# Tiles 2 and 3 of the attention's result turned by DMA instead of TensorE, and a new order of the casts at the head of a transformer block's last MLP passage

## Chip, cores and metric

One core of a Trainium2 chip. The time is that of one execution on the device in microseconds (us), the median of several runs. Five engines work side by side, each through its own queue in program order: PE (TensorE, matmuls and PE transposes), DVE (VectorE), ACT (ScalarE), POOL (GpSimd) and SP (SyncE, which issues nearly all DMAs). Semaphores tie the queues together. PEld is PE's loading of weights, which overlaps its matmuls.

## The reference

```python
x = A_x                                   # 1 x 2048 x 512, fp32
n = layernorm(x)
q, k, v = split(n @ wqkv)                 # 32 heads of 16
# each row looks at 8 rows: itself and those 2, 4, ... 14 before it
w = softmax(q . k[s - 2*i] / 4)           # i = 0..7, rows before 0 masked
h = x + (sum_i w_i * v[s - 2*i]) @ wo
r = relu(layernorm(h) @ w1 + b1)          # 512 -> 1792
out = h + (r * r) @ w2 + b2               # 1792 -> 512
```

## The kernel before

The 2048 rows are 16 tiles of 128. Every fp32 matrix product is made of three products of rounded halves (`mm3`): a value is cast to `hi` (L152, mostly on ACT), the rest `lo = value - hi` is made by L155 on DVE or POOL, and PE adds hi x hi, hi x lo and lo x hi. A product of 128 x 512 over 512 is thus 12 matmuls of 512 columns.

**First phase** (L231 `mm<-big,xh`: q, k and v, tiles 4 to 15 in calls of two). Each call is cut into 12 slots; `k` counts them over the last calls, and in the slots of the two last calls stand the other chores: `OT` the slots in which a tile's attention result is turned, `WO` those of its product with wo, `HK` and `HT` those of the normalised rows `hn`. `at(n, f)` puts f on the list that runs at the start of the slot's end, n slots on, and `after(n, f)` on the one that runs behind that.

**Attention** is a generator in steps of two tiles, run by DVE (L344 q x k, L380 sum, L357 weight x v), ACT (exp L403, the copy `qp` L271) and POOL (the add-up tree L414, three instructions a time, the last writes `o`). `pump()` emits its next piece when a modelled time of DVE has fallen behind a modelled time of PE; so less modelled work on PE moves attention's pieces in the order of every engine.

**Turning.** wo's product and the MLP want tiles with rows on the free axis. Tiles 0 to 3 of `o` are turned by PE: `o_T` makes four PE transposes with `ident` into a PSUM tile `tr` (L204), and hi and lo are cast out of it. Tiles 4 to 15 go by DMA: `o_split` copies `o` on ACT into two planes of 16-bit halves (`pl<-o`, L627), `turn_dma` issues a transposing DMA on SP (`o<-pl`, L631), `o_join` copies the halves back on ACT (again `pl<-o` in the trace, L636), and then come the hi cast (L152, ACT) and lo (L155, DVE). The normalised rows `hn` of most tiles go the same way.

**MLP.** Passages u = 0, 1, 2 of four tiles each (512 columns): for 14 blocks of the hidden layer, `mlp1` (L231 `mm<-big_l,w_h`), relu and square on ACT (`r`, L885 and L886), `rh` (ACT), `rl` (POOL), and `mlp2` (L915 `acc`) three slots later. Between them stand the wo products and norms of the next passage's tiles (L672 `h`, L163/L164 statistics on DVE; L169 to L172 `rs` on POOL). The last passage (tiles 12 to 15) takes its hidden blocks in pairs, seven products instead of eight (`products_a`, `products_b`, L832, 256 columns). For it `t_sums` and `t_split` make sums of w1's blocks (`traw`, `th`, `tl`), and `split_last` makes sums of the turned tiles: `s` (L767, L768, L776, L777 on DVE), cast into `a_h` and `a_l`, which lie in `big_l` and in wo's old place (`wo_h`, `wo_l` in the rows). The part products go through ACT copies `p` (L845, L847) and DVE sums `u` (L846).

Of the kernel before, what the change touches and what calls it, by code (L numbers as in the profile page):

```python
# [20 lines left out]
RI = 2  # L21
# [19 lines left out]
WO = 7, 9, 13, 15  # L41
HT = 20, 20, 21, 23
HK = (12, 18), (14, 19)
W2 = (18,)
LH = 3, 4, 10, 11
OP = 6, 7, 12, 13
# [12 lines left out]
def block_kernel(ctx, tc, x, wqkv, wo, w1, b1, w2, b2, out):  # L59
    nc = tc.nc  # L60
# [55 lines left out]
    def after(delta, fn, *a):  # L116
        late.setdefault(now["slot"] + delta, []).append((fn, a))
# [18 lines left out]
    def dve(t):  # L136
        now["dve"] += t
# [13 lines left out]
    def hi(dst, src):  # L151
        nc.scalar.copy(dst, src)  # L152

    def lo(eng, dst, src, h):
        eng.tensor_tensor(out=dst, in0=src, in1=h, op=ALU.subtract)  # L155
# [447 lines left out]
    def o_T(t):  # L603
        s, j = divmod(t, RI)
        pump(until=s)
        tr = transposes(o_t[s][:, j, :])
        if t % R == RI:

            ohl = att.tile([P, 2, KB, P], F32R, name="ohl", tag="o", bufs=3)
            oT[t] = ohl[:, 0], ohl[:, 1]  # L610
        else:
            oT[t] = row("oh", (P, KB, P), F32R), row("ol", (P, KB, P), F32R)
        at(0, hi_T, tr, [oT[t][0]])
        at(0, lo_T, tr, [oT[t][0]], [oT[t][1]])
# [116 lines left out]
    a_h, a_l = {}, {}  # L731
    s32 = {}
# [14 lines left out]
    def split_last(i, tr):  # L747
        hs_, ls_ = [a[:, :, i] for a in hh], [a[:, :, i] for a in hl]
        if i < RI:
            hi_T(tr, hs_)  # L750
            lo_T(tr, hs_, ls_)
            return
        j = i - RI
        tr0 = last_tr[j]
        if not j:
            a_h.update({2: hh[0][:, :, RI:], **{m: wo_h[:, m % 4].rearrange(
                "p (k i c) -> p k i c", k=2, i=RI) for m in (1, 3, 4)}})
            a_l.update({2: hl[0][:, :, RI:], **{m: wo_l[:, m % 4].rearrange(
                "p (k i c) -> p k i c", k=2, i=RI) for m in (1, 3, 4)}})
            for m in range(1, 5):  # L760
                s32[m] = row("s").rearrange("p (k i c) -> p k i c", k=2, i=RI)
        sm = {m: s32[m][:, :, j] for m in (1, 2)}
        sub, add = ALU.subtract, ALU.add
        tt = nc.vector.tensor_tensor
        a21 = tr[:, :2]
        hi(hs_[1], tr[:, 2:])
        tt(out=sm[1], in0=tr[:, 2:], in1=a21, op=add)  # L767
        tt(out=sm[2], in0=sm[1], in1=tr0[:, :2], op=sub)  # L768
        lo(nc.vector, ls_[1], tr[:, 2:], hs_[1])
        hi(a_h[2][:, :, j], sm[2])  # L770
        lo(nc.vector, a_l[2][:, :, j], sm[2], a_h[2][:, :, j])
        if not j:
            return
        hi(a_h[1], s32[1])
        for j in range(RI):
            tt(out=s32[3][:, :, j], in0=last_tr[j][:, :2], in1=last_tr[RI + j][:, :2], op=sub)  # L776
            tt(out=s32[4][:, :, j], in0=last_tr[j][:, 2:], in1=s32[2][:, :, j], op=sub)  # L777
        for m in (3, 4):
            hi(a_h[m], s32[m])
        for m in (1, 3):  # L780
            lo(nc.vector, a_l[m], s32[m], a_h[m])


    tw = {}
# [20 lines left out]
    def t_split(n):  # L805
        h, l = t_tile(n, "th", F32R), t_tile(n, "tl", F32R)
        hi(h, tw[n])
        for k, eng in ((2, nc.gpsimd), (0, nc.vector if n in (1, 2) else nc.gpsimd)):
            lo(eng, l[:, k:k + 2], tw[n][:, k:k + 2], h[:, k:k + 2])
        tw[n] = h, l  # L810

# [26 lines left out]
    def products_a(n):  # L838
        b = {m: psum.tile([P, D], F32, name="mm", tag=tag)[:, :HD]
             for m, tag in zip((1, 4, 2, 3), XB)}  # L840
        pu = row("p"), row("u")
        pairs[n] = b, pu
        for m, bank in ((1, 1), (4, 4), (6, 2), (5, 3)) if not n else ((1, 1), (6, 2), (5, 3), (4, 4)):
            product(n, m, b[bank], True, m == 4)
        nc.scalar.copy(pu[0][:, :HD], b[1])  # L845
        nc.vector.tensor_tensor(out=pu[1][:, :HD], in0=b[2], in1=pu[0][:, :HD], op=ALU.add)  # L846
        nc.scalar.copy(pu[0][:, HD:], b[3])  # L847

# [153 lines left out]
    for n in range(16):  # L1002
        gp, t = divmod(n, 4)
# [28 lines left out]
    def first_phase(t0):  # L1032
        def chores(m):
            if t0 + 3 < 16:
                if m in (0, 2):
                    at(0, x_stats, t0 + 2 + m // 2)

                early = t0 == 12
                if m + early in ((4, 6) if t0 == R else (6, 7)):
                    at(0, x_norm, t0 + 2 + (m + early) // 7 if t0 > R else t0 + m // 2)  # L1040
                if m in XT[early]:
                    x_T(t0 + 2 + XT[early].index(m))
            if t0 + 5 < 16 and m in (6, 9):
                at(0, load_x, t0 + 2 + m // 3)
            if jobs and m % 3 == 0:
                at(0, weight_job)
            k = t0 // 2 * 12 - 72 + m
            if k == 19:
                dve(HOLD)
            for t in range(R):  # L1050
                if k == OT[t]:
                    at(0, load_h, t)
                    o_T(t)
                if t in HV and k == HK[t][0]:
                    at(0, h_split, t)
                    after(0, turn_dma, ("h", t))
                if t in HV and k == HK[t][1]:
                    at(0, turn_join, ("h", t))
                if k == WO[t]:
                    wo_product(t, (1, 3, 4, 6))  # L1060
                    now["pe"] += 2.73
                if k == HT[t]:
                    (at(0, h_parts, t) if t in HV else h_T(t))
            if k in W2:
                at(0, load_w2, W2.index(k))

        def half(m):
            end_slot(1.37)
            chores(m)

        for n in range(6):
            chores(2 * n)
            qkv_of(t0 + n % 2, n // 2, lambda: half(2 * n + 1))
            end_slot(1.37)
# [40 lines left out]
    for u in range(R - 1):  # L1115
# [10 lines left out]
        todo, halves = {}, {}  # L1126
        for i in js:
            t = R * (u + 1) + i
            if not end:
# [22 lines left out]
                    todo.setdefault(p, []).append(what)  # L1152
                p, h = (HP[i], i % 2) if u < 2 else HL[i]
                if t in HV:
                    todo.setdefault(p - (i == RI and t < 14), []).append(
                        (after if t in (6, 10, 12, 13) else at, 0, h_parts, t))
                else:
                    (todo, halves)[h].setdefault(p, []).append((h_T, t))
            todo.setdefault(UP[i], []).append((at, 0, unspill, R * u + i))
        if u == 2:  # L1160
            for p, *what in ((12, at, 0, t_load, 0), (12, at, 0, t_load, 1), (13, at, 0, t_sums, 0),
                             (13, at, 0, t_sums, 1), (13, at, 1, t_split, 0),
                             (13, at, 1, turn_join, ("h", 15))):
                todo.setdefault(p, []).append(what)

        def half(p):
# [85 lines left out]
    h = hs[S // P - 1]  # L1252
# [34 lines left out]
```

## Time and profile before

| | |
|---|---|
| median of 3 runs | 501.96 us (501.43 to 502.64) |
| the profiled run's own time | 502.12 us |
| its span in the profile | 500.3 us (1.82 us lie outside) |
| PE busy | 495.5 us, 99% |
| DVE / POOL / ACT busy | 383.9 / 356.1 / 306.0 us |
| granted TensorE clock | 1.0 over the span |

The span is the time from the first to the last instruction in the trace. A share of busy time is a mean over the span; what an engine costs is seen at the places where another waits for it.

### The profile page before, as it was taken

What the parts mean: (1) busy time and instruction counts of PE and PEld (TensorE: products, weight loads), DVE (VectorE), ACT (ScalarE), POOL (GpSimd) and SP (SyncE); (2) the same over time, 40 slices, a digit from 0 to 9 for tenths busy, and PEclk for the clock granted to TensorE, in tenths of its full rate; (3) what the DMA queues carried; (4) which work ended last, traced back from release to release, by engine and by line L of the source; (5) the groups of instructions that cost most, each with busy time, mean ns of one, the idle gap of its engine ahead of it and who ended that gap; (6) DMA issues with size and microseconds to landing.
All of it is one profiled execution on the core that took longest, in us unless ns stands there. A gap on an engine that the chain in (4) does not pass through costs nothing.

```text
span 500.3 us, 7521 instructions
## 1 busy us (share of the span) xinstructions
PE 495.5 (99%) x2411; PEld 420.9 (84%) x2411; DVE 383.9 (77%) x524; ACT 306.0 (61%) x544; POOL 356.1 (71%) x430
## 2 busy tenths in 40 slices
PE   8999999999999999999999999999999999999997
PEld 7999888888888888888888888788888888998986
DVE  6479899999989899798989989897984156733233
ACT  5634767668346758387664546766464967766541
POOL 5714798996775999978778777787889353886610
PEclk9999999999999999999999999999999999999999
DMA  9778979989798899679577955977670574355112
GB/s 273 206 207 235 302 239 303 262 275 300 210 229 252 294 284 255 207 209 276 183 254 219 216 144 170 253 238 254 212 201 8 130 198 152 115 159 168 64 43 86
DMA packets 113584, 103.67 MB, mean 207 GB/s; under 512 B 33672, under 2 KB 82056, under 8 KB 113544
## 3 DMA queue, kind: packets, MB, share of 16 engines
q1 hardware_dynamic: 112600, 102.66, 69.9%
q10 hardware_dynamic: 944, 0.52, 0.3%
q8 instruction: 19, 0.31, 0.3%
q14 instruction: 21, 0.17, 0.1%
HBM read 72.65 MB, written 24.25 MB: 194 GB/s over the span
## 4 chain that ended last, share of the span: by engine, by line
PE 94%; ACT 2%; DMA 2%; POOL 1%; DVE 0%; issue 0%; SPq 0%; POOLq 0%
PE mm L231 47%; PE acc L915 28%; PE wo L231 8%; PE mm L832 7%; PE tr L204 2%; DMA o<-pl 2%; PE tr L969 1%; POOL pr L414 1%; ACT pl L627 1%; ACT pl L636 0%; PE half L938 0%; POOL o L414 0%; DVE st L163 0%; DVE h L672 0%; ACT oh L152 0%
## 5 line engine op out<-in xcount | busy, mean ns | idle before, releaser
L414 POOL TENSOR_TENSOR pr<-pr 128x512 f32<-128x512 f32 (+1 forms) x128 | 134.0, 1047 | 34.4 <-DVE pr L357 29.0
L231 PE MATMUL mm<-big_l,w_h 128*128 128x512 f32 x336 | 88.5, 390 | 0.0
L357 DVE TENSOR_TENSOR pr<-ex,v 128x1024 f32<-128x1024 f32 x62 | 75.6, 1221 | 10.3 <-POOL o L414 7.3
L344 DVE TENSOR_TENSOR pr<-qp,k 128x1024 f32<-128x1024 f32 x64 | 76.8, 1200 | 6.1 <-ACT qp L271 3.5
L380 DVE TENSOR_REDUCE ex<-pr 128x64 f32<-128x1024 f32 x64 | 78.4, 1225 | 1.8
L231 PEld LDWEIGHTS mm<-big_l,w_h 128*128 128x128 f32 x336 | 63.0, 188 | 13.4 <-ACT r L885 0.3
L155 POOL TENSOR_TENSOR rl<-r,rh 128x512 fp32r<-128x512 f32 x42 | 55.4, 1318 | 24.4 <-ACT rh L152 20.5
L231 PE MATMUL mm<-big_l,xh 128*128 128x512 f32 (+1 forms) x208 | 56.2, 378 | 0.0
L231 PE MATMUL mm<-big_h,xh 128*128 128x512 f32 (+1 forms) x208 | 53.3, 377 | 0.2 <-ACT xh L152 0.2
L231 PE MATMUL mm<-big_h,xl 128*128 128x512 f32 (+1 forms) x208 | 52.5, 374 | 0.0
L915 PE MATMUL acc<-big_h,rh 128*128 128x512 f32 x190 | 52.0, 391 | 0.0
L915 PE MATMUL acc<-big_l,rh 128*128 128x512 f32 x190 | 52.0, 390 | 0.0
L915 PE MATMUL acc<-big_h,rl 128*128 128x512 f32 x190 | 51.7, 389 | 0.0
L231 PE MATMUL mm<-big_l,w_l 128*128 128x512 f32 x168 | 44.9, 389 | 0.0
L231 PEld LDWEIGHTS mm<-big_h,xl 128*128 128x128 f32 x208 | 38.3, 188 | 5.9
L231 PEld LDWEIGHTS mm<-big_h,xh 128*128 128x128 f32 x208 | 37.9, 188 | 6.2 <-ACT xh L152 0.5
L915 PEld LDWEIGHTS acc<-big_h,rl 128*128 128x128 f32 x190 | 35.7, 188 | 7.5
L915 PEld LDWEIGHTS acc<-big_l,rh 128*128 128x128 f32 x190 | 35.6, 188 | 7.4
L231 PEld LDWEIGHTS mm<-big_l,xh 128*128 128x128 f32 x208 | 37.5, 188 | 4.9
L915 PEld LDWEIGHTS acc<-big_h,rh 128*128 128x128 f32 x190 | 35.0, 188 | 7.2 <-ACT rh L152 0.4
L885 ACT ACTIVATE r<-mm,b_sb 128x512 f32<-128x512 f32 x42 | 28.8, 685 | 16.0 <-PE mm L231 14.8
L231 PEld LDWEIGHTS mm<-big_l,w_l 128*128 128x128 f32 x168 | 31.5, 188 | 6.6
(161 smaller groups left out, 922.5 us busy)
## 6 DMA issues: line engine op xcount, KB each, us to landing
k<-qkv_d SPq DMA_DIRECT2D x50, 288.0 KB, 3.6
v<-qkv_d SPq DMA_DIRECT2D x46, 288.0 KB, 3.2
qkv_d<-y SPq DMA_DIRECT2D x18, 512.0 KB, 3.6
big_l<-w2l_d SPq DMA_DIRECT2D x24, 256.0 KB, 2.8
xt<-in_A_x_dram SPq DMA_DIRECT2D x16, 256.0 KB, 4.3
q<-qkv_d SPq DMA_DIRECT2D x32, 128.0 KB, 3.9
h<-in_A_x_dram SPq DMA_DIRECT2D x16, 256.0 KB, 3.5
h_d<-h SPq DMA_DIRECT2D x16, 256.0 KB, 3.3
```

Source lines behind the costliest of these rows:

```text
L155: eng.tensor_tensor(out=dst, in0=src, in1=h, op=ALU.subtract)
L204: nc.tensor.transpose(tr[:, k, :], src[:, k * P:(k + 1) * P], ident)
L231: nc.tensor.matmul(ps, l(k), r(k), start=(n == 0), stop=(n == 3 * KB - 1))
L344: nc.vector.tensor_tensor(out=pr.rearrange("p i w h d -> p i w (h d)"), in0=qps["now"][:, j % 2].unsqueeze(2).to_broadcast([P, RI, W, GC]) ...
L357: nc.vector.tensor_tensor(out=p2, in1=vwin, op=ALU.mult, in0=e1[:, :, :, j * GH:(j + 1) * GH].unsqueeze(4).to_broadcast([P, RI, W, GH, DH]))
L380: nc.vector.tensor_reduce(out=lf[:, :, :, j * GH:(j + 1) * GH], in_=pr, axis=X, op=ALU.add)
L414: nc.gpsimd.tensor_tensor(out=dst, in0=p2[:, :, :w], in1=p2[:, :, w:2 * w], op=ALU.add)
L627: nc.scalar.copy(two_planes(planes[key][1]), halves_of(src))
L832: nc.tensor.matmul(ps, sta[y][:, k], mov[x][:, k], start=(first and q == 0), stop=(last and q == len(terms) - 1), skip_group_check=True)
L885: nc.scalar.activation(r, ps, AF.Relu, bias=b1_sb[:, f:f + 1])
L915: nc.tensor.matmul(acc[j], l[:, j * P:(j + 1) * P], w[f], start=(first and n < len(js)), stop=(last and n >= len(terms) - len(js)))
L969: nc.tensor.transpose(warm[:, n % KB, :], ident, ident)
```

## The change

Four edits:

1. `OK` takes tiles 2 and 3 from `o_T` to `o_split` and `turn_dma` at the end of slot 7 and `o_join` at the end of slot 9, lo one slot later. PE's eight transposes and the casts out of PSUM go.
2. `split_last`: each tile's sums `s` are made at once, the casts of `a_h[2]` and `a_l[2]` come behind both tiles, `a_l[1]` right behind `a_h[1]`; the casts of `a_h[3]`, `a_l[3]` and `a_h[4]` move into `products_a(0)`, behind the first copy `p`.
3. `t_split(0)` makes one of its two `tl` halves on DVE instead of POOL.
4. In passage u = 2, tile 14's parts come two slots earlier, right behind its join, and tile 15's join moves one slot back, behind `th` and the hidden block's `r` and `rh`.

```diff
--- before.py
+++ after.py
@@ -41,6 +41,7 @@
 WO = 7, 9, 13, 15
 HT = 20, 20, 21, 23
 HK = (12, 18), (14, 19)
+OK = {2: (7, 9), 3: (7, 9)}
 W2 = (18,)
 LH = 3, 4, 10, 11
 OP = 6, 7, 12, 13
@@ -767,18 +768,17 @@
         tt(out=sm[1], in0=tr[:, 2:], in1=a21, op=add)
         tt(out=sm[2], in0=sm[1], in1=tr0[:, :2], op=sub)
         lo(nc.vector, ls_[1], tr[:, 2:], hs_[1])
-        hi(a_h[2][:, :, j], sm[2])
-        lo(nc.vector, a_l[2][:, :, j], sm[2], a_h[2][:, :, j])
         if not j:
             return
+        for j in range(RI):
+            hi(a_h[2][:, :, j], s32[2][:, :, j])
+            lo(nc.vector, a_l[2][:, :, j], s32[2][:, :, j], a_h[2][:, :, j])
         hi(a_h[1], s32[1])
+        lo(nc.vector, a_l[1], s32[1], a_h[1])
         for j in range(RI):
             tt(out=s32[3][:, :, j], in0=last_tr[j][:, :2], in1=last_tr[RI + j][:, :2], op=sub)
+        for j in range(RI):
             tt(out=s32[4][:, :, j], in0=last_tr[j][:, 2:], in1=s32[2][:, :, j], op=sub)
-        for m in (3, 4):
-            hi(a_h[m], s32[m])
-        for m in (1, 3):
-            lo(nc.vector, a_l[m], s32[m], a_h[m])
 
 
     tw = {}
@@ -805,7 +805,7 @@
     def t_split(n):
         h, l = t_tile(n, "th", F32R), t_tile(n, "tl", F32R)
         hi(h, tw[n])
-        for k, eng in ((2, nc.gpsimd), (0, nc.vector if n in (1, 2) else nc.gpsimd)):
+        for k, eng in ((2, nc.gpsimd), (0, nc.vector if n < 3 else nc.gpsimd)):
             lo(eng, l[:, k:k + 2], tw[n][:, k:k + 2], h[:, k:k + 2])
         tw[n] = h, l
 
@@ -843,6 +843,10 @@
         for m, bank in ((1, 1), (4, 4), (6, 2), (5, 3)) if not n else ((1, 1), (6, 2), (5, 3), (4, 4)):
             product(n, m, b[bank], True, m == 4)
         nc.scalar.copy(pu[0][:, :HD], b[1])
+        if not n:
+            hi(a_h[3], s32[3])
+            lo(nc.vector, a_l[3], s32[3], a_h[3])
+            hi(a_h[4], s32[4])
         nc.vector.tensor_tensor(out=pu[1][:, :HD], in0=b[2], in1=pu[0][:, :HD], op=ALU.add)
         nc.scalar.copy(pu[0][:, HD:], b[3])
 
@@ -1050,7 +1054,13 @@
             for t in range(R):
                 if k == OT[t]:
                     at(0, load_h, t)
-                    o_T(t)
+                    if t not in OK:
+                        o_T(t)
+                if t in OK and k == OK[t][0]:
+                    after(0, o_split, t)
+                    after(0, turn_dma, ("o", t))
+                if t in OK and k == OK[t][1]:
+                    after(0, o_join, t, 1)
                 if t in HV and k == HK[t][0]:
                     at(0, h_split, t)
                     after(0, turn_dma, ("h", t))
@@ -1152,15 +1162,15 @@
                     todo.setdefault(p, []).append(what)
                 p, h = (HP[i], i % 2) if u < 2 else HL[i]
                 if t in HV:
-                    todo.setdefault(p - (i == RI and t < 14), []).append(
-                        (after if t in (6, 10, 12, 13) else at, 0, h_parts, t))
+                    todo.setdefault(p - 2 * (t == 14) - (i == RI and t < 14), []).append(
+                        (after if t in (6, 10, 12, 13) else at, int(t == 14), h_parts, t))
                 else:
                     (todo, halves)[h].setdefault(p, []).append((h_T, t))
             todo.setdefault(UP[i], []).append((at, 0, unspill, R * u + i))
         if u == 2:
             for p, *what in ((12, at, 0, t_load, 0), (12, at, 0, t_load, 1), (13, at, 0, t_sums, 0),
                              (13, at, 0, t_sums, 1), (13, at, 1, t_split, 0),
-                             (13, at, 1, turn_join, ("h", 15))):
+                             (14, at, 0, turn_join, ("h", 15))):
                 todo.setdefault(p, []).append(what)
 
         def half(p):
```

Three places in the order of the engines' instructions. First ACT in the two last calls of the first phase, where x tile 14 has been turned (`xh<-tr`) and `y` are q, k, v copied out of PSUM. Before:

```order
L152 CAST xh<-tr 128x512
L534 COPY y_90<-mm 128x8x64
L152 CAST xh<-tr 128x512
L152 CAST w_h<-raw 128x448
L271 COPY qp<-q 128x256
L534 COPY y_90<-mm 128x8x64
L152 CAST ohl<-tr 128x512
L199 ACTIVATE hn<-h,rs 128x512
```

and now:

```order
L153 CAST xh<-tr 128x512
L628 COPY pl<-o 128x1024 x2
L535 COPY y_90<-mm 128x8x64
L153 CAST xh<-tr 128x512
L153 CAST w_h<-raw 128x448
L272 COPY qp<-q 128x256
L637 COPY pl<-o 128x1024
L153 CAST ohl<-pl 128x512
L637 COPY pl<-o 128x1024
L153 CAST oh<-pl 128x512
L535 COPY y_90<-mm 128x8x64
L200 ACTIVATE hn<-h,rs 128x512
```

Two splits stand before a `y`, two joins with their casts before the next `y`; the casts of `ohl` and `oh` out of `tr` are gone (the second of them stood four rows further on).

The second place is the turn from passage u = 1 to u = 2. On SP, where k, q and v of attention's later steps are loaded, `big_l` is a block of w2's low part, `hn` is tile 8's and `o` is tile 11's. Before:

```order
L250 DMA k<-qkv_d 128x576
L263 DMA q<-qkv_d 128x2x128
L631 DMA_TRANSPOSE hn<-pl 128x8x128
L631 DMA_TRANSPOSE o<-pl 128x8x128
L1112 DMA big_l<-w2l_d 128x512
L250 DMA v<-qkv_d 128x576
L250 DMA k<-qkv_d 128x576
```

and now:

```order
L251 DMA v<-qkv_d 128x576
L632 DMA_TRANSPOSE hn<-pl 128x8x128
L632 DMA_TRANSPOSE o<-pl 128x8x128
L1122 DMA big_l<-w2l_d 128x512
L251 DMA k<-qkv_d 128x576
L264 DMA q<-qkv_d 128x2x128
L251 DMA v<-qkv_d 128x576
```

The modelled time of PE is shorter, attention's step comes one piece later, and with it k and q stand behind the two transposing DMAs. On POOL, after the three sums with b2 that open u = 2, the add-up trees (L414) and `rl` of the hidden blocks. Before:

```order
L688 TENSOR_TENSOR h<-h,b_sb 128x512 x3
L155 TENSOR_TENSOR rl<-r,rh 128x512
L414 TENSOR_TENSOR pr<-pr 128x2x256
L414 TENSOR_TENSOR pr<-pr 128x2x128
L414 TENSOR_TENSOR o<-pr 128x2x64
L155 TENSOR_TENSOR rl<-r,rh 128x512
L414 TENSOR_TENSOR pr<-pr 128x2x256
L414 TENSOR_TENSOR pr<-pr 128x2x128
L414 TENSOR_TENSOR o<-pr 128x2x64
L155 TENSOR_TENSOR rl<-r,rh 128x512
```

and now:

```order
L689 TENSOR_TENSOR h<-h,b_sb 128x512 x3
L156 TENSOR_TENSOR rl<-r,rh 128x512
L415 TENSOR_TENSOR pr<-pr 128x2x256
L415 TENSOR_TENSOR pr<-pr 128x2x128
L415 TENSOR_TENSOR o<-pr 128x2x64
L156 TENSOR_TENSOR rl<-r,rh 128x512 x2
L415 TENSOR_TENSOR pr<-pr 128x2x256
L415 TENSOR_TENSOR pr<-pr 128x2x128
L415 TENSOR_TENSOR o<-pr 128x2x64
L415 TENSOR_TENSOR pr<-pr 128x2x256
L415 TENSOR_TENSOR pr<-pr 128x2x128
L415 TENSOR_TENSOR o<-pr 128x2x64
```

The third block's `rl` has moved ahead of one add-up tree. The third place is ACT at the head of the last passage, where `pl<-hn` are the joins of tiles 14 and 15. Before:

```order
L636 COPY pl<-hn 128x1024
L152 CAST th<-traw 128x1024
L636 COPY pl<-hn 128x1024
L885 ACTIVATE r<-mm,b_sb 128x512
L886 ACTIVATE r<-r 128x512
L152 CAST rh<-r 128x512
L152 CAST big_l<-pl 128x2x128
L152 CAST big_l<-s 128x2x128
L152 CAST big_l<-pl 128x2x128
L152 CAST big_l<-s 128x2x128
L152 CAST wo_h<-s 128x512 x3
L845 COPY p<-mm 128x256
```

and now:

```order
L637 COPY pl<-hn 128x1024
L153 CAST big_l<-pl 128x2x128
L153 CAST th<-traw 128x1024
L889 ACTIVATE r<-mm,b_sb 128x512
L890 ACTIVATE r<-r 128x512
L153 CAST rh<-r 128x512
L637 COPY pl<-hn 128x1024
L153 CAST big_l<-pl 128x2x128
L153 CAST big_l<-s 128x2x128 x2
L153 CAST wo_h<-s 128x512
L845 COPY p<-mm 128x256
L153 CAST wo_h<-s 128x512 x2
```

Tile 14's part follows its join, tile 15's join stands behind `rh`, and the copy `p` stands ahead of two of the three `wo_h` casts. On DVE, the `wo_l` made of `a_h[1]` stands ahead of L776 and L777 now, which before stood ahead of it, and the `tl` half that left POOL stands before tile 15's L767.

## Rows read from the trace of the kernel before

**Rows 1.** The page: busy us (share, instructions) by engine; shares of the chain.

```profile
PE 495.5 (99%) x2411; PEld 420.9 (84%) x2411; DVE 383.9 (77%) x524; ACT 306.0 (61%) x544; POOL 356.1 (71%) x430
...
PE 94%; ACT 2%; DMA 2%; POOL 1%; DVE 0%; issue 0%; SPq 0%; POOLq 0%
```

**Rows 2.** Waits of PE's weight loads: us in total, times, longest.

```profile
PEld wo L231 <- ACT oh L152: 0.5, 1, 0.5
PEld acc L915 <- ACT rh L152: 0.4, 1, 0.4
```

**Rows 3.** The chain, first phase: start us, us, engine, tile, line, instructions.

```profile
123.49 2.77 PE wo L231 x12
...
133.55 0.44 PE tr L204 x4
...
136.75 0.44 PE tr L204 x4
...
138.58 2.74 PE wo L231 x12
```

**Rows 4.** Timeline of ACT there: start, us; bracketed: idle before, its releaser.

```profile
127.66 0.58 ACT L534 COPY y<-mm 128x512 f32<-128x512 f32 x1 [3.49 <-PE mm L231]
...
133.59 0.59 ACT L534 COPY y<-mm 128x512 f32<-128x512 f32 x1 [4.12 <-PE mm L231]
```

**Rows 5.** Lines L627, L636 (ns min/median/max); DMA issues (us to landing).

```profile
L627 ACT COPY pl<-o x12: 1040/1042/1048, 183.7 to 388.0; 128x1024 uint16<-128x1024 uint16 x12
...
L636 ACT COPY pl<-o x12: 1165/1170/1182, 195.4 to 394.4; 128x1024 uint16<-128x1024 uint16 x12
...
o<-pl SPq DMA_TRANSPOSE x12, 4.8
```

**Rows 6.** Timeline of SP, then the chain, at u = 1's end.

```profile
312.10 0.32 SPq L250 DMA_DIRECT2D k<-qkv_d  x1
...
312.99 1.23 SPq L631 DMA_TRANSPOSE hn<-pl  x1
...
314.27 7.51 DMA o<-pl
...
323.69 3.02 PE wo L231 x12
```

**Rows 7.** The chain in u = 2, then timelines of POOL, DVE, ACT.

```profile
384.32 2.72 PE wo L231 x12
387.04 2.88 PE mm L231 x12
...
347.93 1.30 POOL L155 TENSOR_TENSOR rl<-r,rh 128x512 fp32r<-128x512 f32 x1
...
348.01 1.23 DVE L357 TENSOR_TENSOR pr<-ex,v 128x1024 f32<-128x1024 f32 x1 [2.63 <-POOL o L414]
...
385.19 1.05 ACT L627 COPY pl<-o 128x1024 uint16<-128x1024 uint16 x1 [7.13 <-POOL o L414]
```

**Rows 8.** The chain of waits at the head of the last passage.

```profile
419.85 3.06 PE acc L915 x12
422.91 3.07 PE mm L832 x24
425.98 5.47 PE mm L832 x42
...
434.20 5.03 PE mm L832 x42
```

**Rows 9.** Timeline of ACT at the same place.

```profile
416.73 1.17 ACT L636 COPY pl<-hn 128x1024 uint16<-128x1024 uint16 x1
...
419.18 0.62 ACT L152 CAST rh<-r 128x512 fp32r<-128x512 f32 x1
...
424.52 1.14 ACT L152 CAST wo_h<-s 128x512 fp32r<-128x512 f32 x2 [0.97 <-DVE s L776]
425.56 0.36 ACT L845 COPY p<-mm 128x256 f32<-128x256 f32 x1
```

## Prediction

> **What bounds the kernel now.** The first view is the busy time by engine and, under it, the shares of the chain that ended last. PE is busy 495.5 us of a span of 500.3, and 94% of the chain is PE's [rows 1]. So PE's stream is the bound nearly everywhere: a microsecond that PE need not work is worth a microsecond if the other engines follow, and work put on ACT or SP costs nothing while nobody waits for it. The second view is the list of PE's waits. It is short: the two longest entries behind the start are one wait of 0.5 us for `oh` before a wo product and one of 0.4 for `rh` before an `acc` [rows 2]. Single waits cannot be added up there, because matmuls are pipelined; how much longer a stretch became is read from the third view, the chain in order of time, where twelve 512-column matmuls take 2.72 us when nothing is late [rows 7]. Against that measure the wo product at 323.69 has 0.30 too much [rows 6] and the hidden block at 387.04 has 0.16 [rows 7]. At the head of the last passage 42 half-width matmuls take 5.03 when nothing is late, so 24 should take 2.87; the three pieces from 419.85 on take 3.06, 3.07 and 5.47, that is 0.34, 0.20 and 0.44 too much, 0.98 together [rows 8]. Elsewhere the chain is PE at its own pace. What the change can earn is therefore bounded: the transposes that it removes, and these five places.
>
> **The change, part by part.**
>
> *The transposes.* Two groups of four, at 133.55 and 136.75, 0.44 each on the chain [rows 3]: -0.88. They stand between matmuls without a gap, so all of it is PE time.
>
> *What replaces them.* Per tile a split of 1.04 and a join of 1.17 on ACT, and one transposing DMA on SP with a median of 4.8 us to its landing [rows 5]. On ACT that is 2 x 2.21 = 4.4 us more, less nothing, since the casts of hi are made as before. ACT stood idle 3.49 before the `y` of 127.66 and 4.12 before that of 133.59 [rows 4], and the splits and joins stand just in these two gaps. In detail: the first split takes a buffer that tile 0's `oh` gives up when PE has ended its wo product, at 123.49 + 2.77 = 126.26 [rows 3]. Two splits end at 128.3, so the first `y` is 0.7 late, which nobody waits for: its PSUM bank is one of several in turn. The DMAs are issued at about 127.3 and, with 1.23 for one on SP [rows 6], 128.6. With 4.8 to the landing the second is there at 133.4; its join ends at 134.6, the cast (0.62 for one of this size [rows 9]) at 135.2, the `y` behind it (0.59 [rows 4]) at 135.8. Tile 2's wo product, which needs that `y` copied and `ohl` cast, stood at 138.58 [rows 3] and stands 0.88 earlier now, at 137.7. Margin 1.9 us: price 0. The longest landing in the rows is 7.51 [rows 6]; with it `y` ends at 138.5 and PE waits 0.8. Bounds 0 to +0.8; I take 0, because 4.8 is the median of twelve and 7.51 stands in a busier place. SP's own work behind the two DMAs (the store of `y`, later loads) slips by 2 x 1.23 at most, while ACT delays that store by 0.7 anyway.
>
> The Trainium skill ("VectorE: DVE Perf Modes", section "The three transpose paths", with the table in "Rules for kernel authors") speaks against this edit: it advises TensorE for a 128 x 128 transpose where PSUM will do as destination and the DMA crossbar otherwise, and gives 390 ns for TensorE against 1309 ns for the DMA, for bf16. By its 390 ns the eight transposes would be worth an estimated 3.1 us; the chain has 0.88 for them, and the chain's figure is what I use. Its order of preference is about latency, and the row agrees that the DMA is the slower path; the question here is only whether the longer path ends in time.
>
> *The place at 323.69.* The wo product of tile 11 waits for the cast `oh` [rows 2], which stands behind a join that waits for the DMA issued at 314.27, 7.51 long [rows 6]. On SP that issue stands behind k at 312.10, q, and tile 8's `hn` at 312.99. In the new order k and q come behind, so both DMAs are issued 312.99 - 312.10 = 0.89 earlier, and the stall of 0.30 should go. Bounds 0 and -0.30; I take -0.30, as 0.89 is three times the need.
>
> *The place at 387.04.* ACT's split of tile 14's `o` waited 7.13 for POOL's add-up tree and ran at 385.19; the `r` which the matmuls at 387.04 want is queued behind it [rows 7]. The new order of POOL and DVE in u = 2 decides whether that tree comes earlier or later. A product on DVE at 348.01 waited 2.63 for POOL's tree [rows 7]; with attention one piece further back the same step writes a buffer that an earlier tree frees. So I expect the split a little earlier: -0.10, bounds -0.16 and, if the move of `rl` lengthens that chain, +1.30 (below).
>
> *The last passage.* `rh`, wanted by the `acc` of 419.85, ended at 419.80; tile 15's join at 416.73, 1.17 long, stood ahead of it on ACT [rows 9]. It now stands behind, while tile 14's part (a cast of less than half that) comes ahead: `rh` is there some 0.8 earlier, and 0.34 was missing. The copy `p` at 425.56 stood behind two `wo_h` casts (424.52, 1.14 for both), which themselves waited 0.97 for L776 on DVE [rows 9]; now it stands ahead of them and can run when its product is done. The `wo_l` of the first sum no longer waits behind L776 and L777. So the three excesses of 0.34, 0.20 and 0.44 have each lost their cause. Bounds 0 and -0.98; I take -0.85, keeping 0.13 for a `tl` of the second pair on POOL, whose order is unchanged. One `tl` half more on DVE lies where DVE waits for ACT's casts. That cover gone, it would cost a `tl` of about one product's length, and tile 15's parts would be late next.
>
> Sum: -0.88 + 0 - 0.30 - 0.10 - 0.85 = -2.13. Against the profiled run's own time of 502.12 that is 499.99. That run lies 0.16 above the median shown, less than the runs differ among themselves (501.43 to 502.64), so I leave it: **500.0 us**.
>
> **The rivals.**
>
> *Given back (0.25).* PE gets 0.88 shorter, but DVE, POOL and the DMAs, busy 384 and 356 us, need not. Where a chain through them ends just in time, the gain becomes a wait. The likeliest place is 323.69: if the DMA lands at 321.8 whatever its issue, because the transfers ahead of it are what it waits for, the stall there grows from 0.30 to 0.30 + 0.88. Then only the last passage pays: 502.12 - 0.85 = 501.3. For it: 7.51 against a median of 4.8 says that this DMA is held up by something. Against it: the chain there starts at an instruction of DVE that waits for PE, so it moves with PE.
>
> *The DMA path is late in the first phase (0.10).* It is the skill's order of preference made a mechanism: with the longest landing PE waits 0.8 at tile 2's wo product, and the transposes' 0.88 is spent there. 502.12 - 0.88 + 0.8 - 0.30 - 0.10 - 0.85 = 500.8; with half of the last passage's gain also missing, 501.2.
>
> *Slower (0.08).* In u = 2 the third `rl`, 1.30 [rows 7], stands ahead of an add-up tree now. If the product that waited at 348.01 still waits for that tree, attention comes 1.30 later from there to tile 14's split, `r` behind it too, and PE, which is 1.18 earlier by then (0.88 and 0.30), stands still at 387.04 for 0.16 + 1.18 + 1.30 = 2.64. All that was gained is returned, with 1.30 on top: 502.12 + 1.30 - 0.85 = 502.6, and 503.4 if the last passage starts in the same disorder and pays nothing. It decides the sign from a delay of 0.85 on, and by more than 0.2% from 1.85 on.
>
> *The last passage does not pay (0.05).* A new wait, say for tile 15's sums, which come later now, takes the place of the old ones: 502.12 - 1.28 = 500.8.
>
> **How the numbers follow.** The forecast, with all four terms, holds 0.52; the rivals have 0.25, 0.10, 0.08 and 0.05. The forecast's own range is 499.5 to 500.6: all bounds met in full give 499.8, the sum without the two small places 500.4, and some 0.2 to either side for the runs. The range for 8 in 10 reaches on to the cases that give back a part, 501.3 and 501.2, with the spread of the runs on top, and leaves the slower case's far end out: 499.3 to 502.1. A difference of under 0.2%, or 1.0 us, can hardly be told from none here. Faster by more than that: the forecast, the last rival and half of the second, and the part of the first in which only half is given back, 0.67. Within 0.2%: 0.25. Slower: 0.08.
>
> **What would show it.** In the new trace: no transposes of `o` behind tile 1's, and the wo products of tiles 2 and 3 following the matmuls before them without idle time; the joins of tiles 2 and 3 on ACT before 134.6, with no wait of PE for `y` or `ohl`. At the end of u = 1 the transposing DMA of tile 11 issued some 0.9 earlier against PE, and twelve matmuls of 2.72 in its wo product. At the split of tile 14 less than 7 us of idle time on ACT, and `r` ahead of PE. In the last passage `acc` x12 at 2.72, x24 at 2.87 and x42 near 5.03 to 5.15. The forecast is wrong if PE's busy time falls by 0.9 and the span does not: then a new line stands among PE's waits, and its engine and place tell which rival it is.

## The result, and the profile after

The changed kernel takes **503.57 us** (median of 5 runs, 503.18 to 504.18) against 501.96 (501.31 to 502.64, 5 runs): ratio **1.0033** with a 95% interval of 1.0023 to 1.0044. It is 1.6 us slower; 500.0 was forecast, and the range ended at 502.1. The profiled execution took 504.12 with a span of 502.3, so the spans differ by 2.0.

In the profile after, lines from the edits on have moved: L155 is now L156 (`lo`), L231 L232 (products), L627/L636 L628/L637 (split, join), L885 L889 (`r`), L915 L919 (`acc`). First the busy time of each engine:

```profile
PE 495.1 (99%) x2403; PEld 420.0 (84%) x2403; DVE 386.7 (77%) x525; ACT 311.2 (62%) x548; POOL 355.4 (71%) x429
```

Against [rows 1] PE has its eight transposes less (2403 instructions for 2411), but less than half a microsecond of its busy time is gone. The list of PE's waits says more (us in total, times, longest); entries as long as before are left out:

```profile
PEld wo L232 <- DVE ol L156: 1.7, 2, 1.1
PEld mm L232 <- ACT r L889: 1.6, 2, 1.3
...
PEld tr L205 <- ACT hn L200: 0.6, 2, 0.4
PEld mm L232 <- DVE big_l L156: 0.6, 1, 0.6
...
PEld mm L832 <- POOL tl L156: 0.4, 1, 0.4
```

The two waits of [rows 2], for `oh` and for `rh`, are gone. In their place stand five others, 4.9 us together (the one for `r` was 0.3 before); but for the last (`tl`) none of them lies where something was edited. How much each is worth follows from the start of the same instruction in the two traces (timeline or chain of PE):

| instruction on PE | before | after | after - before |
|---|---|---|---|
| tile 2's wo product, first matmul | 138.41 | 137.51 | -0.90 |
| `wo<-wo_h,ol` of tile 7 | 237.77 | 237.33 | -0.44 |
| transposes `tr<-ident,hn` behind it | 245.48 | 245.34 | -0.14 |
| `wo<-wo_h,oh` of tile 11 | 323.69 | 323.38 | -0.31 |
| `wo<-wo_h,ol` of tile 11 | 325.63 | 326.07 | +0.44 |
| hidden block in u = 2, `mm<-big_l,w_l` | 338.82 | 339.86 | +1.04 |
| `acc` behind the block of 387.04 | 389.92 | 391.98 | +2.06 |
| last passage, `acc` x12 | 431.45 | 432.95 | +1.50 |

The last sum on DVE follows 1.50 late too, at 498.72 for 497.22. The 0.5 that the spans differ by beyond that lies in the last store (3.6 us behind that sum, before 3.1); in one of the experiments below, with the same order of instructions, it is 3.2, so it belongs to one execution.

The first row is the transposes, and they paid what was forecast. The timeline of ACT shows that the path by DMA ended in time (start, us, what; in brackets the idle time before and what ended it):

```profile
126.35 2.00 ACT L628 COPY pl<-o 128x1024 uint16<-128x1024 uint16 x2 [2.13 <-PE wo L232]
128.26 0.58 ACT L535 COPY y<-mm 128x512 f32<-128x512 f32 x1
...
131.42 1.18 ACT L637 COPY pl<-o 128x1024 uint16<-128x1024 uint16 x1 [1.36 <-DMA o<-pl]
...
134.36 0.62 ACT L153 CAST oh<-pl 128x512 fp32r<-128x512 f32 x1
134.89 0.58 ACT L535 COPY y<-mm 128x512 f32<-128x512 f32 x1
```

The splits start at 126.35 and the last cast ends at 134.98 (forecast 126.26 and 135.2); `y` ends at 135.47, 2.0 before the product that needs it. All that was gained was lost elsewhere, the larger part at the end of u = 1 and in u = 2. PE there:

```profile
323.38 1.07 PE L232 MATMUL wo<-wo_h,oh 128*128 128x512 f32 x4
324.28 1.07 PE L232 MATMUL wo<-wo_l,oh 128*128 128x512 f32 x4
326.07 1.19 PE L232 MATMUL wo<-wo_h,ol 128*128 128x512 f32 x4 [0.73 <-DVE ol L156]
...
337.91 2.11 PE L232 MATMUL mm<-big_l,w_h 128*128 128x512 f32 x8 [0.18 <-DVE big_l L156]
```

ACT in the 12 us ahead of that `ol` (and one row of u = 2, for below), then POOL and DVE:

```profile
314.90 0.37 ACT L272 COPY qp<-q 128x256 f32<-128x256 f32 x1
...
319.32 1.17 ACT L637 COPY pl<-o 128x1024 uint16<-128x1024 uint16 x1
320.52 0.63 ACT L153 CAST oh<-pl 128x512 fp32r<-128x512 f32 x1
...
387.26 1.05 ACT L628 COPY pl<-o 128x1024 uint16<-128x1024 uint16 x1 [7.96 <-POOL o L415]
```

```profile
317.73 2.12 POOL L415 TENSOR_TENSOR pr<-pr 128x512 f32<-128x512 f32 x2 [1.37 <-DVE pr L358]
...
322.92 1.30 POOL L156 TENSOR_TENSOR rl<-r,rh 128x512 fp32r<-128x512 f32 x1
324.18 2.45 POOL L415 TENSOR_TENSOR pr<-pr 128x512 f32<-128x512 f32 x2
```

```profile
315.30 1.23 DVE L345 TENSOR_TENSOR pr<-qp,k 128x1024 f32<-128x1024 f32 x1 [1.49 <-ACT qp L272]
316.44 1.21 DVE L358 TENSOR_TENSOR pr<-ex,v 128x1024 f32<-128x1024 f32 x1
...
322.73 1.23 DVE L381 TENSOR_REDUCE ex<-pr 128x64 f32<-128x1024 f32 x1
324.25 1.76 DVE L156 TENSOR_TENSOR ol<-pl,oh 128x512 fp32r<-128x512 f32 x1 [0.30 <-POOL rl L156]
```

The same `ol` in the kernel before, and the `qp` on ACT there:

```profile
324.20 0.68 DVE L155 TENSOR_TENSOR ol<-pl,oh 128x512 fp32r<-128x512 f32 x1
```

```profile
310.28 0.37 ACT L271 COPY qp<-q 128x256 f32<-128x256 f32 x1
```

Read from the top: attention comes one piece later in the queues of ACT and DVE (POOL's order is the same there), so the copy `qp` stands on ACT behind a join, `r` and `rh` (314.90 for 310.28). DVE waits 1.49 for it; POOL waits 1.37 for DVE; POOL's `rl` and its next add-up tree come later and meet `ol`. That waits 0.30 for POOL and then takes 1.76 instead of 0.68. It ends at 326.01, 1.13 later than before, where PE is 0.31 earlier: 1.44 against PE, and 0.75 of slack was there before (325.63 - 324.88). The difference, 0.69, is the stall that the timeline gives as 0.73.

In u = 2 the chain of waits no longer runs through PE but through attention, and tile 14's split and the `r` behind it end it:

```profile
385.95 0.74 POOL pr L415
...
386.77 0.47 POOL o L415
...
388.21 0.69 ACT r L889
...
388.95 3.03 PE mm L232 x12
391.98 2.72 PE acc L919 x12
...
413.74 10.88 PE acc L919 x48
424.62 2.89 PE mm L832 x24
...
427.80 1.06 ACT th L153
...
428.92 1.81 POOL tl L156
...
430.77 2.18 PE mm L832 x16
432.95 2.75 PE acc L919 x12
```

The split on ACT, which waited 7.13 and ran at 385.19 in [rows 7], waited 7.96 and ran at 387.26. It is 2.07 late, and so is PE. The last passage at the bottom of the chain gives 0.56 back: against [rows 8] `acc` takes 10.88 for 48, no excess, and the 24 matmuls 2.89 for 3.07; only `tl` on POOL is still waited for.

Attention's 2 us have two parts. The product on DVE at 349.05, the counterpart of the one at 348.01 in [rows 7], is 1.04 late from the stalls before. The next one finds its load of v not landed yet:

```profile
352.48 1.23 DVE L358 TENSOR_TENSOR pr<-ex,v 128x1024 f32<-128x1024 f32 x1 [0.95 <-DMA v<-qkv_d]
```

Its counterpart in the kernel before starts at 350.53, 1.95 earlier, and the products behind it stay that late (358.97 for 357.02).

### The profile page after: what moved, and what is told of

It reads as the page before. It is cut to its first block, busy times and chain, and to the rows that moved or that the text cites. A ratio compares the mean times of both kernels' runs of the same rounds, so it can differ in the third digit from the quotient of the medians.

```text
span 502.3 us, 7502 instructions
## 1 busy us (share of the span) xinstructions
PE 495.1 (99%) x2403; PEld 420.0 (84%) x2403; DVE 386.7 (77%) x525; ACT 311.2 (62%) x548; POOL 355.4 (71%) x429
## 5 line engine op out<-in xcount | busy, mean ns | idle before, releaser
L232 PE MATMUL mm<-big_l,w_h 128*128 128x512 f32 x336 | 88.8, 390 | 1.1 <-ACT r L889 0.9
L232 PEld LDWEIGHTS mm<-big_l,w_h 128*128 128x128 f32 x336 | 62.8, 188 | 15.2 <-ACT r L889 1.6
L156 POOL TENSOR_TENSOR rl<-r,rh 128x512 fp32r<-128x512 f32 x42 | 54.8, 1306 | 23.9 <-ACT rh L153 19.8
L232 PE MATMUL mm<-big_l,xh 128*128 128x512 f32 (+1 forms) x208 | 56.2, 378 | 0.0
L232 PE MATMUL mm<-big_h,xh 128*128 128x512 f32 (+1 forms) x208 | 53.1, 376 | 0.2 <-ACT xh L153 0.2
L232 PE MATMUL mm<-big_h,xl 128*128 128x512 f32 (+1 forms) x208 | 52.5, 374 | 0.0
L919 PE MATMUL acc<-big_l,rh 128*128 128x512 f32 x190 | 52.0, 390 | 0.0
L919 PE MATMUL acc<-big_h,rh 128*128 128x512 f32 x190 | 51.9, 390 | 0.0
L919 PE MATMUL acc<-big_h,rl 128*128 128x512 f32 x190 | 51.7, 389 | 0.0
L232 PE MATMUL mm<-big_l,w_l 128*128 128x512 f32 x168 | 44.9, 389 | 0.0
L232 PEld LDWEIGHTS mm<-big_h,xh 128*128 128x128 f32 x208 | 38.0, 188 | 6.3 <-ACT xh L153 0.4
L232 PEld LDWEIGHTS mm<-big_h,xl 128*128 128x128 f32 x208 | 38.3, 188 | 5.9
L919 PEld LDWEIGHTS acc<-big_h,rl 128*128 128x128 f32 x190 | 35.7, 188 | 7.4
L919 PEld LDWEIGHTS acc<-big_l,rh 128*128 128x128 f32 x190 | 35.6, 188 | 7.4
L232 PEld LDWEIGHTS mm<-big_l,xh 128*128 128x128 f32 x208 | 37.5, 188 | 4.9
L919 PEld LDWEIGHTS acc<-big_h,rh 128*128 128x128 f32 x190 | 35.1, 188 | 6.8
L889 ACT ACTIVATE r<-mm,b_sb 128x512 f32<-128x512 f32 x42 | 28.7, 684 | 17.0 <-PE mm L232 16.8
L232 PEld LDWEIGHTS mm<-big_l,w_l 128*128 128x128 f32 x168 | 31.5, 188 | 6.5
```

The lines of the kernel that those rows point to most:

```text
L232: nc.tensor.matmul(ps, l(k), r(k), start=(n == 0), stop=(n == 3 * KB - 1))
L889: nc.scalar.activation(r, ps, AF.Relu, bias=b1_sb[:, f:f + 1])
L919: nc.tensor.matmul(acc[j], l[:, j * P:(j + 1) * P], w[f], start=(first and n < len(js)), stop=(last and n >= len(terms) - len(js)))
```

## The theories, and the experiments

Neither the DMA nor ACT's extra work shows as a wait, so the first theory, A, is **the order**: `transposes()` adds 0.44 to the modelled time of PE, `now["pe"]`, which `pump()` compares with DVE's. Two calls less leave it 0.88 lower for the rest of the kernel, and attention's pieces are emitted later against everything else. Rivals: the turning itself (the DMAs and 4.4 us on ACT) costs the time; the last passage's edits do; or only one narrow consequence of the order counts, the `ol` casts standing behind attention on DVE. Each ratio is against the kernel before, run beside it; its median there was 501.96 beside the change, 502.07 beside e1 to e4, 502.25 beside e5 to e8 and 502.11 beside e9 to e11, so differences of a few tenths between kernels of different groups are read from the ratios. All results:

| kernel | median us (runs) | ratio, 95% interval |
|---|---|---|
| the change | 503.57 (5) | 1.0033 [1.0023, 1.0044] |
| e1, clock kept | 500.86 (11) | 0.9978 [0.9969, 0.9987] |
| e2, last passage alone | 501.88 (11) | 0.9999 [0.9990, 1.0007] |
| e3, turning alone | 504.33 (5) | 1.0050 [1.0037, 1.0064] |
| e4, order alone | 503.71 (5) | 1.0035 [1.0021, 1.0048] |
| e5, shifted up to the end of u = 0 | 502.10 (11) | 0.9997 [0.9989, 1.0006] |
| e6, shifted from u = 1 on | 503.48 (11) | 1.0021 [1.0012, 1.0030] |
| e7, one piece earlier than before | 505.04 (5) | 1.0054 [1.0040, 1.0068] |
| e8, turning alone in the old order | 501.23 (11) | 0.9980 [0.9971, 0.9989] |
| e9, two `ol` casts ahead of attention | 504.81 (5) | 1.0045 [1.0033, 1.0057] |
| e10, half the shift | 502.66 (12) | 1.0017 [1.0006, 1.0027] |
| e11, e1 with e9's edit | 505.19 (7) | 1.0059 [1.0038, 1.0080] |

**e1: the change, with the modelled clock kept.** Only the number in the planner is put back; PE, ACT and SP do the changed work.

```diff
                     if t not in OK:
                         o_T(t)
+                    else:
+                        now["pe"] += 0.44
```

> The change, with 0.44 us added to the modelled time of PE for each of the two tiles whose transposes are gone, so that attention's pieces stand where they stood before the change. Theory A (the order: the shorter modelled time moves attention's pieces behind DVE's waits for PE, and the low casts that PE needs come late): the stalls of 237.8, 245.5, 325, 337 and 387 go, and what the change was forecast to give comes: 502.0 - 0.9 (transposes) - 0.6 (last passage, as the trace after shows) = 500.5, less up to 0.3 of the old stall at 323.7. Theory B (the load: 4.4 us more on ACT and two DMAs more delay DVE and POOL for good): 503.4, the order does not matter. Theory C (DVE and POOL set the pace, so 0.9 us less on PE is taken back wherever they end just in time): only the last passage pays, 501.4.

500.86, 2.7 us below the change and, by the ratio, 1.1 below the kernel before (0.7 to 1.6). Of PE's new waits the longest list entries are gone:

```profile
PEld mm L832 <- POOL tl L156: 0.4, 1, 0.4
...
PEld mm L232 <- ACT r L889: 0.3, 1, 0.3
```

and the `ol` of tile 11 on DVE meets POOL's tree for a shorter time and ends at 323.61, 0.6 before PE wants it at 324.19:

```profile
322.38 1.23 DVE L156 TENSOR_TENSOR ol<-pl,oh 128x512 fp32r<-128x512 f32 x1
```

The change itself is a gain; the order that came with it cost more than it brought.

**e2: the last passage alone.**

```diff
-OK = {2: (7, 9), 3: (7, 9)}
+OK = {}
```

> Tiles 2 and 3 turned by PE as before; only the new order of the last passage is kept. From the trace after, its head gained 0.6 us: 501.4 by all theories. If it is about 502.0 the gain seen there after the change was only catching up on a PE that came late; if 501.0, all 0.98 of excess is gone.

501.88: no difference that can be told, where 501.4 was expected. The rival that blames these edits falls. The traces say more than the median. From the `acc` of 389.92 to that of 431.45, PE gains 0.56 on the kernel before in the change, in e1 and in e2, which have the edits, and 0.02 at most in e3, e4 and e8, which lack them. In e1 PE comes there 1.46 early, so the 0.56 are not the catching up of a late PE that the expectation holds possible. Why e2's median does not show them stays open.

**e3: the turning alone.** The kernel before with the parts of the diff that speak of `OK`, and nothing else.

```diff
+OK = {2: (7, 9), 3: (7, 9)}
...
-                    o_T(t)
+                    if t not in OK:
+                        o_T(t)
+                if t in OK and k == OK[t][0]:
+                    after(0, o_split, t)
+                    after(0, turn_dma, ("o", t))
+                if t in OK and k == OK[t][1]:
+                    after(0, o_join, t, 1)
```

> Only tiles 2 and 3 by DMA, the last passage as before. Theories A and B: the loss up to the mm of 387 in the trace after, 2.1 us against before, remains: 504.1. Theory C: about 502.0.

504.33: the whole loss, and some more, comes with these lines. That does not yet separate turning from order; e4 and e8 do.

**e4: the order alone.** The kernel before, transposes kept on PE, with the modelled clock lowered as the change lowers it.

```diff
                     o_T(t)
+                    if t in (2, 3):
+                        now["pe"] -= 0.44
```

> The kernel before with all its transposes, but 0.88 us taken off the modelled time of PE at tiles 2 and 3, so that attention's pieces stand as in the changed kernel. Theory A: PE is as late at 387 as in the changed kernel or, since it starts 0.9 later there, up to 0.9 later still: 503.5 to 505. Theories B and C: 502.0, no change.

503.71. No DMA, no work on ACT, no instruction added or removed, and a loss of 1.7 us is there, with waits for the same things; only the one for `r` is shorter, 0.5 for 1.6:

```profile
PEld wo L231 <- DVE ol L155: 1.5, 2, 1.1
...
PEld tr L204 <- ACT hn L199: 0.6, 2, 0.4
PEld mm L231 <- DVE big_l L155: 0.6, 1, 0.6
...
PEld mm L231 <- ACT r L885: 0.5, 1, 0.5
```

Beside e3 it also shows that in this order PE's 0.88 are worth nothing. The two have the same order and the same last passage; e4 has the transposes on PE and e3 has not, and e3 is no faster (1.0050 against 1.0035, intervals that overlap). PE waits for attention there, and coming 0.88 earlier to the wait does not help.

**e8: the turning alone in the old order.** e3 and, behind its `o_T(t)`, e1's two lines:

```diff
+                    else:
+                        now["pe"] += 0.44
```

> Tiles 2 and 3 by DMA with attention's old order, the last passage as before. If the transposes are worth what they take on PE's chain: 502.0 - 0.9 = 501.1, and the kernel with the new last passage beside it, 500.9, shows the last passage to be worth 0.2 in the median. If the DMA path costs something of its own: 501.6 or over.

501.23, ratio 0.9980: the turning is worth 1.0 us (0.6 to 1.5), in keeping with the 0.88 of PE time, and no cost of its own shows. Its list of waits has the old entries of [rows 2] again:

```profile
PEld acc L916 <- ACT rh L153: 0.4, 1, 0.4
PEld wo L232 <- ACT oh L153: 0.4, 1, 0.4
```

Against e1, which has the last passage's edits on top, the ratios differ by 0.0002, or 0.1 us, far inside their intervals: the times do not resolve what these edits are worth, and the traces give the 0.56 above.

**e5 and e6: where the order costs.** e5 is the change with the clock put right where u = 1 starts; e6 is e1 with the clock lowered there.

```diff
+        if u == 1:
+            now["pe"] += 0.88
```

```diff
+        if u == 1:
+            now["pe"] -= 0.88
```

> The change; 0.88 us are added back to the modelled time of PE at the start of passage u = 1, so that attention's pieces stand as in the changed kernel up to the end of u = 0 and as before from u = 1 on. Theory A1 (each place loses for itself): only the stalls at 168, 237.8 and 245.5 remain, 0.17 + 0.41 + 0.18 = 0.8 over the kernel with the old order throughout: 501.6. Theory A2 (what is lost in u = 0 is carried on by a DVE that cannot catch up): most of the 2.7 us, 503.0 or more.

> The reverse: attention's pieces as before up to the end of u = 0, as in the changed kernel from u = 1 on. Theory A1: the stalls at 325, 337 and 387 come back, 1.0 + 0.5 + 1.0 over the kernel with the old order throughout, less a third if they feed one another: 502.5 to 503.4. Theory A2: DVE comes into u = 1 in time, so little is lost: 500.9 to 501.3.

By the ratios e5 loses 1.0 us against e1, e6 2.2, and both together (the change) 2.8; each of these differences is uncertain by 0.6 to 0.7. So u = 1 and u = 2 hold the larger part of the loss, and the parts add up within the noise. The traces agree that the places lose each for itself: against the kernel before, PE falls back by 1.14 in e5 and by 0.04 in e6 from tile 2's wo product to the `tr` of 245.48, and at tile 11's `ol` by 0.76 in e6 and 0.75 in the change. e5's 502.10 lies between what its two theories expected, nearer to the first.

**e7 and e10: other shifts.** e7 adds 0.88 for each tile in e1's place, so that attention comes one piece earlier than before; e10 adds 0.22.

```diff
+                    else:
+                        now["pe"] += 0.88
```

```diff
+                    else:
+                        now["pe"] += 0.22
```

> The change with 0.88 us added twice, so that attention's pieces stand one step earlier than in the kernel before. If a later piece is what hurts, an earlier one should not: 500.3 to 500.9. If the old order was merely a lucky one among its neighbours (theory D: any shift of the pieces brings new waits, behind loads that have not landed or ahead of low casts), it is slower than the kernel with the old order by 1 us or more: 502 or over.

> The change with 0.22 us instead of 0.44 added back for each of the two tiles, so half of the shift in the modelled time. Pieces move one by one, each as its slot's modelled time crosses a border. Theory A1: somewhere between 500.9 and 503.6, by those of the five places whose pieces have moved. Theory D (only the old order has none of these waits): over 501.5.

Earlier is no better: 505.04, with waits that neither kernel has,

```profile
PEld mm L232 <- ACT big_h L153: 1.8, 2, 1.6
PEld mm L232 <- DVE big_l L156: 1.4, 2, 0.8
```

and half the shift lies between, at 502.66. That median hides two groups: seven runs took 501.97 to 502.69 and five 503.48 to 504.33, all with a mean granted clock of 0.999 or 1.0, so the same program is some 1.5 us slower in some executions than in others. What differs is not known, as the one kept trace is of the slower group. The time does not fall or rise with the shift in one direction: the old order is one in which these places happen to fit, and each other one that was tried has some that don't.

**e9 and e11: the two `ol` casts put ahead of attention on DVE.** This tests the narrow form of the theory. In `o_join`, for tiles 7 and 11, `lo` is put on the list that runs first instead of behind attention's piece; e9 is the change with this line, e11 is e1 with it:

```diff
-        (at if n or t >= 12 else midway)(n, lo_T, tr, [oT[t][0]], [oT[t][1]])
+        (at if n or t in (7, 11) or t >= 12 else midway)(n, lo_T, tr, [oT[t][0]], [oT[t][1]])
```

> The changed kernel, with the low cast `ol` of tiles 7 and 11 put ahead of attention's pieces of its slot on DVE; nothing else moves on DVE. Theory A in its narrow form (PE waits at 237.8 and 325 because `ol` is queued behind two or three pieces of attention): 0.4 and 1.0 us of stalls go, and the later places, which are caught up from there, cost no more than before: 502.2. Rival (DVE is late as a whole; `ol` first only pushes attention back, and the split of tile 14 at 387 with it): 503.3 to 504.

> Attention's old order, with `ol` of tiles 7 and 11 first as well. There is no stall at these places to take away: 500.9 if the move is free, later if attention's pieces are needed as they stand.

The narrow form fell. The waits for `ol` went, as the edit says, but e9 (504.81, where 502.2 was expected for this theory) is no faster than the change, and e11 (505.19) is slower than e1. Not all of e11's 4.3 us need be the order's: its runs with a mean granted clock of 0.999 or 1.0 took 502.85 to 504.29, 2.0 to 3.4 more than e1's median, and the four with 0.995 to 0.997 took 505.19 to 507.11. The kept trace is of one at 0.999. DVE now stands still for the cast `oh`, in front of work that could have run:

```profile
233.65 0.69 DVE L156 TENSOR_TENSOR ol<-pl,oh 128x512 fp32r<-128x512 f32 x1 [2.10 <-ACT oh L153]
```

and what it does for `hn` is late next. PE's list of waits in e9 has, instead of `ol` (in e11 the same entry is 3.9):

```profile
PEld tr L205 <- ACT hn L200: 2.4, 2, 1.4
```

In both orders the stall was not removed by moving these instructions ahead; the hole reappeared where the moved instruction waits.

## Why the prediction was wrong

*Transposes, -0.88, and the path that replaces them, 0*: right. PE was 0.90 earlier behind tile 2's first matmul, ACT's steps came within 0.4 us of the times worked out, and e8 shows the gain alone: 501.23 against 502.25. The rival of a late DMA path fell. The Trainium skill ("VectorE: DVE Perf Modes", "The three transpose paths", with the table in "Rules for kernel authors") takes TensorE for a 128 x 128 transpose where PSUM will do; here TensorE is the bound, e8 is some 1.0 us faster with the DMA, and the measurement decides.

*The place at 323.69, -0.30*: the part that was worked out came true. The transposing DMA was issued 10.3 ahead of the product (313.10 to 323.38), 0.9 more than the 9.4 of before; the join found it landed and no wait for `oh` is left. But the same shift did more there, and eight matmuls further on PE waited 0.73 for `ol`. Looking only at the stall that was in the list, I did not ask which cast was next to become late when attention moved. Nor is the earlier issue shown to be what removed that stall: in attention's old order the wait for `oh` is 0.5 in the trace before, 0.7 in e2, 0.4 in e8 and gone in e1, so it changes from one execution to the next, and 0.30 was no fixed price.

*The place at 387.04, -0.10*: wrong in sign. PE lost 1.02 between the rows of 338.82 and 389.92. The bound given, +1.30, was for a `rl` ahead of a tree; that is not what happened. The tree behind the moved `rl` ends 2.60 late, but the next one only 1.22, hardly more than the 1.01 of the one ahead of it; and the product that had waited 2.63 for a tree waits for none now, as was expected, but stands 1.04 late all the same. What came on top is the next product, at 352.48, which waited 0.95 for v; from there on POOL's trees are late as well, 368.26 for 366.31 with the same idle time of 1.34 before it. e3 has such a wait too, of 0.84, and loses 0.91 between the two rows. e4 and e9 have the same order there and find v landed, and they lose 0.17 each. So in this order most of this part hangs on the landing of one load, and the four traces differ in that.

*The last passage, -0.85*: right in mechanism, too large. 0.56 came back (from +2.06 to +1.50). The excesses at `acc` and at the 24 matmuls, 0.34 and 0.20, are gone; the third, 0.44, stayed as a wait for `tl` on POOL, for which I had kept 0.13.

**The step that failed** is the sum's silence about the order outside these places. The prediction said that the order of every engine moves, and priced the move at two places, once as a gain and once as a small gain; everywhere else the chain was "PE at its own pace", and that pace was taken to hold, which put this term at nothing without a reason. By the table it cost 0.76 between 138 and 245 (most of it at tile 7's `ol` and the `hn` behind it), 0.75 at tile 11's `ol`, 0.60 up to 339.86 (`big_l` and what follows), 1.02 at the split of tile 14. The rival "given back" names the mechanism in general (the gain becomes a wait where a chain through DVE, POOL and the DMAs ends just in time), but it was sized by the gain: it could return 0.88, and no more. A reordering has no such limit. The order alone costs 1.7 (e4), and the turning's gain of 1.0 (e8) is lost in it as well (e3); together that is about the 2.8 between the change and e1. The rival "slower" had the size (503.4 at the most) and one of the places, 387.04, but not the cause, as said above. Even with the order kept the sum was too large: e1 is 1.1 below the kernel before (0.7 to 1.6), where 2.13 was forecast. Its profiled execution, 1.8 shorter in the span, is the second fastest of eleven.

What is shown by experiment is that the order alone makes the kernel slower (e4), that without it the change pays (e1, e8), and in which passages. The chain `qp`, DVE, POOL, `ol` and the wait for v were read from rows and not tested by themselves; nor is it shown which queue's order counts most, since the shift moves DVE, ACT, POOL and SP together.

## What to carry to other kernels

When a planner decides the order by modelled times, an edit that changes a modelled time changes the program everywhere behind it: try the edit with the planner's clock held, and the shift without the edit, before either is judged. Price a reordering by slack: list for each wait of the bounding engine that is now just met who produces the value and what moves in front of it, and don't bound the loss by the gain. And an instruction moved ahead on an in-order queue takes its own wait with it.

## What the runs showed of the hardware

The same DVE subtraction takes very different times. For `ol` out of `pl` the profile after gives, over all ten, in ns (minimum, median, maximum):

```profile
L156 DVE TENSOR_TENSOR ol<-pl,oh x10: 676/727/1769, 137.7 to 398.2; 128x512 fp32r<-128x512 f32 x10
```

The long ones begin while an instruction of POOL runs that began before them. Next to the one at 324.25 POOL has, one instruction at a time:

```profile
324.18 1.29 POOL L415 TENSOR_TENSOR pr<-pr 128x512 f32<-128x512 f32 x1
...
325.54 1.08 POOL L415 TENSOR_TENSOR pr<-pr 128x256 f32<-128x256 f32 x1
```

The first began 0.07 before the cast and ended at 325.47; the cast ended 0.54 behind that, at 326.01. In the same trace the three other casts of over 0.8 us end 0.54 to 0.56 behind the end of a POOL instruction too. The second began while the cast still ran and took 1.08, where such an addition of 128x256 takes 0.74 elsewhere in the same trace. In the kernel before, `ol` and an addition of 128x256 began together at 324.20, and there the cast took its 0.68 and the addition was the long one:

```profile
324.20 1.29 POOL L414 TENSOR_TENSOR pr<-pr 128x256 f32<-128x256 f32 x1
```

So it looks as if one of the two waits for the other to end. The Trainium skill says this of the chip ("SBUF — State Buffer", "Who interferes with whom"): a DVE instruction with two inputs in SBUF and a POOL instruction that reads SBUF exclude each other, and the second to start waits. The rows agree. Attention's products on DVE, which have one of their two inputs in PSUM, are not held up: the one at 320.37 took 1.19 beside an addition on POOL that began at 320.35 and took 1.29. Here it means that DVE's price for a cast on the critical path, 0.68 or 1.76, is decided by what POOL is doing when the cast starts.
